# Attention scores in matmuls of 512 and 256 columns instead of 384, and a later ready time for TensorE's operands in the planner

## The chip, the core and the metric

The kernel runs on one core of a Trainium2 chip. The metric is the device time of one execution in microseconds (us). The profile names the engines PE (TensorE matmuls), PEld (TensorE weight loads), DVE (VectorE), ACT (ScalarE), POOL (GpSimd) and SP (SyncE, which issues DMAs). PSUM, where matmuls write, is one array of 8 banks of 512 fp32 columns here, called `banks`.

## What is computed

Attention of 24,576 queries (two batches of 12,288) over 768 keys each, which are 4x4 averages of `kv` times `w_sr`; keys and values are the same. Two feed-forward layers follow, the first with ELU, the second with squared ReLU, both 128 -> 2048 -> 128.

```python
kv_pool = kv.reshape(B, H // r, r, W // r, r, C).mean(axis=(2, 4))
k = v = kv_pool.reshape(B, -1, C) @ w_sr          # 2 x 768 x 128
s = scale * (q @ k.transpose(0, 2, 1))
a = exp(s - s.max(-1)); a /= a.sum(-1) + 1e-09
x = a @ v
h = x @ w_in;  g = where(h > 0, h, exp(min(h, 0)) - 1);  y = g @ w_out
h = maximum(y @ w_in2, 0);  out = h * h @ w_out2
```

## The kernel before

The queries are cut into 48 blocks t of 512 tokens (24 in each batch). To keep fp32 accuracy, each large product is done as three matmuls of a type named fp32r: an operand is split into a high part (…H) and a low part (…L), and `products` (lines 262 to 266) does L*H, H*H and H*L, each with 512 columns, into one PSUM bank. High parts are mostly made by ACT, low parts by DVE as the difference.

For each block the steps are:

- **scores(t, s)**, s = 0 to 3: 128 queries against 768 keys, six matmuls (lines 485 to 492) into banks 0 and 1, 384 columns in each bank. The pair of banks is the only place for scores after the first block. Then `row_max` (DVE, line 495), `exps` (ACT, line 499), `recip` (DVE), `normalise` (ACT for even s, POOL for odd s), `turn` (DVE, line 517). When the four are turned, `move` (16 DMAs on SP's queue, line 558) brings the probabilities into `pL`.
- **values(t, j)**, j = 0 to 2: `p_hi` (ACT, line 568) copies a third of `pL` to `turned` as the high part, `p_lo` (DVE, line 572) leaves the low part in `pL`; then six matmuls of 512 columns each (line 574). Of each three, the first two read `turned`, the third reads `pL`. The result is split into xH and xL.
- **hidden(0, t, i)** and **down(0, t, i)**, i = 0 to 15: the first layer, three matmuls of 512 columns each, 0.68 us. Between them `exp` (ACT, line 620), `less_one` (POOL, line 623), `pick` (DVE, line 627), and for each pair of i a split into gH (ACT, line 631) and gL (DVE, line 634).
- **hidden(1, t, i)** and **down(1, t, i)**: the second layer, with `relu` and `square` on ACT, the high part sH on POOL (line 658), the low part sL on DVE (line 662). It runs about two blocks behind the first layer, so that PE alternates between steps of both layers, of scores and of values. A step is one such group of matmuls.

No loop sets the order. `Program.order` (lines 57 to 132) draws up, before anything is issued, one list of all steps by simulating the five engines with a table of costs; each engine then runs its steps in that list's order. A step is ready when the last of its operands is done plus a latency of the producing engine (`LATENCY`, line 25). Each engine takes, among its 24 most urgent steps, the most urgent one, unless another could start over 10 ns earlier. Buffers, PSUM banks included, are kept apart from that: a place is free when its last reader is done (`free`). Line 127 is where the finish of a step (`done`, the latency included) becomes the ready time of its users. The planner's list also holds filler matmuls (line 733) where PE would idle long; all of them stand in the opening.

The keys of a batch are made by `make_keys`: six matmuls of 128 columns for kH/kL and six for vH/vL, and a split of each in two halves of 384 columns (lines 400 to 416).

Of the kernel before, what the change touches and what calls it, by code (L numbers as in the profile page):

```python
# [11 lines left out]
F32R = mybir.dt.float32r  # L12
# [17 lines left out]
class Program:  # L30
# [26 lines left out]
    def order(self, kinds, fill=None):  # L57
# [30 lines left out]
        while any(queue.values()):  # L88
# [47 lines left out]
def kernel(  # L136
# [26 lines left out]
    NB = 512  # L163
    NS = NB // P
    NKEY = (HH // R) * (WW // R)
    KH = NKEY // 2
    NKC = NKEY // P
    NF = DFF // P
    BPB = N // NB
# [44 lines left out]
    kinds["scores0"] = [(("bank", i), ("bank", i + 1)) for i in range(0, 8, 2)]  # L214
    ring("pooled", 1, [P, NKEY])
    for tag in ("kH", "kL", "vH", "vL"):
        ring(tag, 1, [P, 2, KH], F32R)
    ring("prob", 3, [P, NKEY])
    ring("turned", 1, [P, NKC, NB], F32R)
    ring("pL", 1, [P, NKC, NB], F32R)  # L220
# [167 lines left out]
    def make_keys(b, due):  # L388
        kept = [("keep", b, t) for t in range(NKC)]

        def make(x, due):
            ps, hi, lo = (x + "ps", b), (x + "H", b), (x + "L", b)
            scale = SCALE if x == "k" else 1.0

            def chunk(c):
                dst = v_chunk(buf(*ps), c)
# [6 lines left out]
            def lo_half(h):  # L403
                nc.vector.scalar_tensor_tensor(
                    out=buf(*lo)[:, h, :], in0=buf(*ps)[:, h, :KH], scalar=scale, in1=f32(buf(*hi)[:, h, :]),
                    op0=ALU.mult, op1=ALU.subtract,
                )
# [11 lines left out]
        make("v", due + 1000)  # L419

    def v_chunk(x, c):
        return x[:, c // 3, (c % 3) * C:(c % 3 + 1) * C]

# [8 lines left out]
    def pieces(x, a):  # L432
        return x[32 * a:32 * (a + 1), :].rearrange("p (g i) -> p g i", i=32)

    def by_half(x):
        return x.rearrange("p (h c) n -> p h c n", h=2)

    def of_chunks(x):
        return x[:, :, :KH].rearrange("p h (c n) -> p h c n", n=P)

    def split(tag, t, ps, cost, due, after):

# [8 lines left out]
    def attention(t, base):  # L451
# [30 lines left out]
        def softmax(s, due):  # L482
            k = (t, s)

            def scores():
                x = [a[:, s * P:(s + 1) * P] for a in parts("qT", t)]
                ps, kH, kL = buf("scores", *k), buf("kH", b), buf("kL", b)
                for h in range(2):
                    nc.tensor.matmul(ps[:, h, :KH], x[0], kH[:, h, :], start=True, stop=False)  # L489
                    nc.tensor.matmul(ps[:, h, :KH], x[0], kL[:, h, :], start=False, stop=False)  # L490
                for h in range(2):
                    nc.tensor.matmul(ps[:, h, :KH], x[1], kH[:, h, :], start=False, stop=True)  # L492

            def row_max():
                nc.vector.tensor_reduce(out=buf("max", *k), in_=buf("scores", *k)[:, :, :KH], op=ALU.max, axis=AX.XY,
                                        negate=True)

            def exps():
                nc.scalar.activation(  # L499
                    buf("prob", *k).rearrange("p (h k) -> p h k", h=2), buf("scores", *k)[:, :, :KH], AF.Exp,  # L500
                    bias=buf("max", *k), accum_out=buf("sum", *k),
                )

# [17 lines left out]

            def p_transpose():
                for c in range(NKC):
                    nc.tensor.transpose(v_chunk(buf("pps", *k), c), buf("prob", *k)[:, c * P:(c + 1) * P], ident)

            def p_hi():
                nc.scalar.copy(by_half(buf("pH", t))[:, :, :, s * P:(s + 1) * P], of_chunks(buf("pps", *k)))

            def p_lo():
                nc.vector.tensor_sub(by_half(buf("pL", t))[:, :, :, s * P:(s + 1) * P], of_chunks(buf("pps", *k)),  # L530
                                     by_half(f32(buf("pH", t)))[:, :, :, s * P:(s + 1) * P])

            done = [("qTH", t), ("qTL", t)]
            if t % BPB == BPB - 1:
# [236 lines left out]
```

## Time and profile before

| | |
|---|---|
| median of 3 runs | 2573.49 us (2572.44 to 2574.39) |
| profiled execution, its own time | 2575.82 us |
| span of that execution | 2574.0 us |
| PE busy | 2558.7 us (99%), 11,636 matmul records |
| DVE, ACT, POOL busy | 2280.9 (89%), 2103.8 (82%), 1343.5 (52%) us |

The recorded length of a matmul is longer than its turn: a 512-column matmul is recorded as 0.39 us long while the next one starts 0.23 us after it, so busy time alone doesn't show whether PE loses time. The distance from the start of one matmul to the start of the next does. A fp32 matmul that is not fp32r, such as those of the keys, has two records.

### The profile page before, as it was taken

The numbers are of one execution on the slowest core, as the hardware profiler recorded it, in microseconds if no ns is written. First come the engines' busy times: TensorE is split into PE (matmuls) and PEld (weight loads), VectorE is DVE, ScalarE is ACT, GpSimd is POOL, SyncE is SP. The second block draws the span as 40 slices with busy tenths as digits, with TensorE's granted clock in tenths as the row PEclk, the third lists the DMA queues.
The fourth block names the chain that finished last, engine by engine and source line by source line (L and its number), as shares of the span: only waits on it lengthen the run. The fifth ranks groups of instructions, "written<-read, shape, count | busy, mean of one in ns | idle before, by whom it ended". The sixth has DMA issues, their size and how long they took to land.

```text
span 2574.0 us, 35216 instructions
## 1 busy us (share of the span) xinstructions
PE 2558.7 (99%) x11636; PEld 2136.3 (83%) x11636; DVE 2280.9 (89%) x2700; ACT 2103.8 (82%) x3138; POOL 1343.5 (52%) x1318
## 2 busy tenths in 40 slices
PE   9999999999999999999999999999999999999999
PEld 8888888888888888888888888888888888888887
DVE  4999989999899899998899989999999899988985
ACT  5888878888788888888888878888888888887886
POOL 3655545555566556564455545554455445544543
PEclk9999999999999999999999999999999999999999
DMA  8012211122112212121112211121112111211110
GB/s 246 13 33 48 47 34 38 38 59 56 46 41 50 67 45 46 42 61 42 37 34 47 48 34 37 38 57 34 37 33 58 38 38 33 49 43 29 33 30 13
DMA packets 360374, 119.29 MB, mean 46 GB/s; under 512 B 209024, under 2 KB 353024, under 8 KB 360192
## 3 DMA queue, kind: packets, MB, share of 16 engines
q1 hardware_dynamic: 358992, 116.85, 19.3%
q8 instruction: 92, 1.51, 0.3%
q14 instruction: 90, 0.74, 0.1%
q10 hardware_dynamic: 1200, 0.20, 0.0%
HBM read 33.61 MB, written 12.58 MB: 18 GB/s over the span
## 4 chain that ended last, share of the span: by engine, by line
PE 89%; SPq 3%; DVE 3%; DMA 2%; ACT 2%; issue 1%; POOL 0%; ACTq 0%; POOLq 0%; DVEq 0%
PE banks L266 27%; PE banks L265 27%; PE banks L264 27%; SPq L558 3%; PE banks L489 3%; PE banks L490 3%; PE banks L492 3%; DVE sL L662 1%; DMA pL<-turned 1%; DVE gL L634 1%; DVE pL L572 0%; DVE g L627 0%; DMA g<-in_kv_dram 0%; DMA r<-in_moe_w_in_dram 0%; ACT prob L499 0%
## 5 line engine op out<-in xcount | busy, mean ns | idle before, releaser
L623 POOL TENSOR_SCALAR e<-e 128x512 f32<-128x512 f32 x768 | 680.0, 888 | 860.6 <-ACT e L620 859.9
L662 DVE TENSOR_TENSOR sL<-r,sH 128x1024 fp32r<-128x1024 f32 x380 | 596.2, 1569 | 13.5 <-POOL sH L658 12.2
L620 ACT ACTIVATE e<-banks 128x512 f32<-128x512 f32 x768 | 458.7, 599 | 156.6 <-PE banks L266 140.1
L634 DVE TENSOR_TENSOR gL<-g,gH 128x1024 fp32r<-128x1024 f32 x384 | 529.0, 1378 | 59.1 <-ACT gH L631 54.2
L627 DVE SCALAR_TENSOR_TENSOR g<-e,banks 128x512 f32<-128x512 f32 x768 | 507.1, 674 | 78.1 <-POOL e L623 76.1
L658 POOL TENSOR_SCALAR sH<-r 128x1024 fp32r<-128x1024 f32 x380 | 411.2, 1082 | 261.1 <-PE banks L265 202.0
L652 ACT ACTIVATE r<-banks 128x512 f32<-128x512 f32 x768 | 462.6, 603 | 64.2 <-DVE sL L662 29.6
L631 ACT CAST gH<-g 128x1024 fp32r<-128x1024 f32 x384 | 404.3, 1053 | 78.0 <-PE banks L265 41.6
L655 ACT ACTIVATE r<-r 128x1024 f32<-128x1024 f32 x384 | 409.7, 1067 | 10.7
L264 PE MATMUL banks<-xH,wi0L 128*128 128x512 f32 x768 | 300.9, 392 | 0.0
L264 PE MATMUL banks<-yH,wi1L 128*128 128x512 f32 x768 | 300.8, 392 | 0.0
L266 PE MATMUL banks<-gL,wo0H 128*128 128x512 f32 x768 | 299.9, 391 | 0.8 <-DVE gL L634 0.8
L266 PE MATMUL banks<-xL,wi0H 128*128 128x512 f32 x768 | 300.4, 391 | 0.0
L264 PE MATMUL banks<-gH,wo0L 128*128 128x512 f32 x768 | 299.5, 390 | 0.7 <-DVE g L627 0.7
L265 PE MATMUL banks<-xH,wi0H 128*128 128x512 f32 x768 | 299.9, 391 | 0.0
L265 PE MATMUL banks<-gH,wo0H 128*128 128x512 f32 x768 | 299.6, 390 | 0.0
L266 PE MATMUL banks<-yL,wi1H 128*128 128x512 f32 x768 | 299.4, 390 | 0.0
L265 PE MATMUL banks<-yH,wi1H 128*128 128x512 f32 x768 | 299.4, 390 | 0.0
L266 PE MATMUL banks<-sL,wo1H 128*128 128x512 f32 x760 | 297.1, 391 | 0.0
L265 PE MATMUL banks<-sH,wo1H 128*128 128x512 f32 x760 | 296.6, 390 | 0.0
L264 PE MATMUL banks<-sH,wo1L 128*128 128x512 f32 x760 | 295.6, 389 | 0.0
L512 POOL TENSOR_SCALAR prob<-prob,rcp 128x768 f32<-128x768 f32 x102 | 190.9, 1871 | 60.1 <-DVE rcp L506 54.9
(132 smaller groups left out, 4348.6 us busy)
## 6 DMA issues: line engine op xcount, KB each, us to landing
pL<-turned SPq DMA_DIRECT2D x720, 96.0 KB, 2.2
out_dram<-o SPq DMA_DIRECT2D x190, 64.0 KB, 1.9
q<-in_q_dram SPq DMA_DIRECT2D x180, 64.0 KB, 2.3
ld<-in_kv_dram SPq DMA_DIRECT2D x32, 256.0 KB, 3.6
g<-in_kv_dram SPq DMA_DIRECT2D x8, 256.0 KB, 6.8
gH<-in_kv_dram SPq DMA_DIRECT2D x8, 256.0 KB, 6.9
r<-in_moe_w_in_dram SPq DMA_DIRECT2D x3, 511.8 KB, 7.3
ld<-in_moe_w_in_dram SPq DMA_DIRECT2D x3, 511.8 KB, 4.2
```

Of the source, the lines that this page charges most:

```text
L264: nc.tensor.matmul(dst, lhs[1], rhs[0], start=start, stop=False)
L265: nc.tensor.matmul(dst, lhs[0], rhs[0], start=False, stop=False)
L266: nc.tensor.matmul(dst, lhs[0], rhs[1], start=False, stop=stop)
L620: nc.scalar.activation(buf("e", *k), buf(*h), AF.Exp)
L623: nc.gpsimd.tensor_scalar(out=buf("e", *k), in0=buf("e", *k), scalar1=-1.0, scalar2=1.0, op0=ALU.add, op1=ALU.mult)
L627: nc.vector.scalar_tensor_tensor(out=buf("g", *pair)[:, i % 2, :], in0=buf("e", *k), scalar=0.0, in1=buf(*h), op0=ALU.min, op1=ALU.max)
L631: nc.scalar.copy(buf("aH", 0, *pair), buf("g", *pair))
L634: nc.vector.tensor_sub(buf("aL", 0, *pair), buf("g", *pair), f32(buf("aH", 0, *pair)))
L652: nc.scalar.activation(buf("r", *pair)[:, i % 2, :], buf(*h), AF.Relu)
L655: nc.scalar.activation(buf("r", *pair), buf("r", *pair), AF.Square)
L658: nc.gpsimd.tensor_scalar(out=buf("aH", 1, *pair), in0=buf("r", *pair), scalar1=1.0, scalar2=1.0, op0=ALU.mult, op1=ALU.mult)
L662: nc.vector.tensor_sub(buf("aL", 1, *pair), buf("r", *pair), f32(buf("aH", 1, *pair)))
```

## The change

Three edits. The first: `scores` now covers the 768 keys in columns 0 to 511 (bank 0) and 512 to 767 (bank 1), with three matmuls each. They are still six matmuls, 2304 columns in all and six weight loads; the third of the six is now the first to read the low part of the queries (before it was the fifth). What reads scores (`row_max`, `exps`, and in the first three blocks `p_hi`, `p_lo`) reads 768 columns that follow each other, where it read two runs of 384. The second: kH, kL, vH, vL are flat arrays of 768 columns, and are split in parts of 512 and 256 columns, whose ACT and DVE steps wait for four and for two key chunks instead of three and three. The third: in the planner, for steps that start after 130 us of its own clock, an operand from another engine counts for PE as ready 400 ns later. It is an edit of the list alone; no wait is added to the program. The costs in the table are as they were.

```diff
+BULK, AHEAD = 130000.0, 400.0
@@ order
             for u in users.get(n, ()):
-                ready[u] = max(ready[u], now[e] + SAME[e] if self.ops[u][0] == e else done)
+                early = AHEAD if start > BULK and self.ops[u][0] == "pe" and e != "pe" else 0.0
+                ready[u] = max(ready[u], now[e] + SAME[e] if self.ops[u][0] == e else done + early)
@@ make_keys
             def hi_half(h):
-                nc.scalar.activation(buf(*hi)[:, h, :], buf(*ps)[:, h, :KH], AF.Copy, scale=scale)
+                x = spans[h]
+                nc.scalar.activation(buf(*hi)[:, x], flat(buf(*ps))[:, x], AF.Copy, scale=scale)
...
-                op((x + "_hi", b, h), "act", 370, due, partial(hi_half, h), [(x, b, 3 * h + i) for i in range(3)])
+                op((x + "_hi", b, h), "act", 370, due, partial(hi_half, h), [(x, b, c) for c in range(4 * h, min(4 * h + 4, NKC))])
...
+    spans = (slice(0, NB), slice(NB, NKEY))
@@ scores
-                ps, kH, kL = buf("scores", *k), buf("kH", b), buf("kL", b)
-                for h in range(2):
-                    nc.tensor.matmul(ps[:, h, :KH], x[0], kH[:, h, :], start=True, stop=False)
-                    nc.tensor.matmul(ps[:, h, :KH], x[0], kL[:, h, :], start=False, stop=False)
-                for h in range(2):
-                    nc.tensor.matmul(ps[:, h, :KH], x[1], kH[:, h, :], start=False, stop=True)
+                ps, kH, kL = flat(buf("scores", *k)), buf("kH", b), buf("kL", b)
+                for y in spans:
+                    nc.tensor.matmul(ps[:, y], x[0], kH[:, y], start=True, stop=False)
+                    nc.tensor.matmul(ps[:, y], x[0], kL[:, y], start=False, stop=False)
+                    nc.tensor.matmul(ps[:, y], x[1], kH[:, y], start=False, stop=True)
```

How the list moves is seen at three places. Line numbers of the changed kernel are one higher in `products` (265 to 267) and four or five higher further down (scores 494 to 496, exps 503, gH 635). Numbers behind a name tell buffers of one kernel apart and mean nothing across the two.

PE, block 16, around values(16, 0), whose matmuls read `turned` and `pL`. Before:

```order
L264 MATMUL banks<-sH_8073,wo1L 128x512
L265 MATMUL banks<-sH_8073,wo1H 128x512
L266 MATMUL banks<-sL_8090,wo1H 128x512
L264 MATMUL banks<-turned_8140,vL_314 128x512
L265 MATMUL banks<-turned_8140,vH_313 128x512
L266 MATMUL banks<-pL_8021,vH_313 128x512
L264 MATMUL banks<-turned_8140,vL_314 128x512
L265 MATMUL banks<-turned_8140,vH_313 128x512
L266 MATMUL banks<-pL_8021,vH_313 128x512
L264 MATMUL banks<-xH_7702,wi0L 128x512
L265 MATMUL banks<-xH_7702,wi0H 128x512
L266 MATMUL banks<-xL_7708,wi0H 128x512
```

The same place in the changed kernel:

```order
L265 MATMUL banks<-sH_8073,wo1L 128x512
L266 MATMUL banks<-sH_8073,wo1H 128x512
L267 MATMUL banks<-sL_8090,wo1H 128x512
L265 MATMUL banks<-xH_7706,wi0L 128x512
L266 MATMUL banks<-xH_7706,wi0H 128x512
L267 MATMUL banks<-xL_7712,wi0H 128x512
L265 MATMUL banks<-turned_8140,vL_314 128x512
L266 MATMUL banks<-turned_8140,vH_313 128x512
L267 MATMUL banks<-pL_8021,vH_313 128x512
```

A step of hidden(0, 15, ·) now stands ahead of values(16, 0). The same shift by one step stands in block 3, blocks 11 to 22 and blocks 24 to 47; in blocks 4 to 10 values(t, 0) comes nine places later and in block 23 thirteen, with p_hi and p_lo moved later too. In the other blocks p_hi and p_lo keep their places on ACT and DVE.

PE, block 17, around scores(17, 1), which stands behind a step of down(0, 15, ·). Before:

```order
L264 MATMUL banks<-gH_8169,wo0L 128x512
L265 MATMUL banks<-gH_8169,wo0H 128x512
L266 MATMUL banks<-gL_8191,wo0H 128x512
L489 MATMUL banks<-kH_240,qTH_7918 128x384
L490 MATMUL banks<-kL_241,qTH_7918 128x384
L489 MATMUL banks<-kH_240,qTH_7918 128x384
L490 MATMUL banks<-kL_241,qTH_7918 128x384
L492 MATMUL banks<-kH_240,qTL_7962 128x384 x2
```

The same place in the changed kernel:

```order
L494 MATMUL banks<-kH_240,qTH_7916 128x512
L495 MATMUL banks<-kL_241,qTH_7916 128x512
L496 MATMUL banks<-kH_240,qTL_7962 128x512
L494 MATMUL banks<-kH_240,qTH_7916 128x256
L495 MATMUL banks<-kL_241,qTH_7916 128x256
L496 MATMUL banks<-kH_240,qTL_7962 128x256
L265 MATMUL banks<-gH_8172,wo0L 128x512
L266 MATMUL banks<-gH_8172,wo0H 128x512
L267 MATMUL banks<-gL_8194,wo0H 128x512
```

The scores are in 512 and 256 columns, and stand ahead of the step that they stood behind; scores(t, 0) and scores(t, 1) do so in blocks 4 to 23.

ACT, block 17, around exps(17, 0), which frees the two banks for scores(17, 1). Before:

```order
L620 ACTIVATE e_8228<-banks 128x512
L631 CAST gH_8242<-g_8167 128x1024
L499 ACTIVATE prob_8221,sum_8253<-banks,max_8237 128x768
L620 ACTIVATE e_8264<-banks 128x512
L652 ACTIVATE r_8219<-banks 128x512
```

The same place in the changed kernel:

```order
L624 ACTIVATE e_8233<-banks 128x512
L503 ACTIVATE prob_8216,sum_8241<-banks,max_8228 128x768
L635 CAST gH_8251<-g_8164 128x1024
L514 ACTIVATE prob_8216<-prob_8216,rcp_8256 128x768
L624 ACTIVATE e_8275<-banks 128x512
```

exps(17, 0) now stands ahead of the cast of gH, and normalise(17, 0) right behind that. In all, 412 of 3502 steps on PE stand elsewhere, all but the values by three places or fewer; on DVE 506, on ACT 445, on POOL 32. The last blocks' end and the 37 fillers are in the same places.

## Rows read from the trace of the kernel before

**Rows 1.** The page: busy time of each engine; TensorE's granted clock in 40 slices.

```profile
PE 2558.7 (99%) x11636; PEld 2136.3 (83%) x11636; DVE 2280.9 (89%) x2700; ACT 2103.8 (82%) x3138; POOL 1343.5 (52%) x1318
...
PEclk9999999999999999999999999999999999999999
```

**Rows 2.** Stretch: length, busy PE, PEld, DVE, ACT, POOL, clock, DMA share, GB/s.

```profile
1500.00:2000.00 500.00, 499.83 (x2242) 416.99 (x2241) 453.57 (x538) 415.83 (x615) 254.46 (x251) 1.00 0.19 42
```

**Rows 3.** Timeline, PE, 999 to 1012 us: start, length, instruction; 52 rows between.

```profile
999.82 0.39 PE L265 MATMUL banks<-yH,wi1H 128*128 128x512 f32 x1
...
1011.83 0.39 PE L264 MATMUL banks<-turned,vL 128*128 128x512 f32 x1
```

**Rows 4.** Timeline, PE, one tile of scores and nine matmuls behind it.

```profile
1242.89 0.33 PE L489 MATMUL banks<-kH,qTH 128*128 128x384 f32 x1
...
1243.95 0.39 PE L264 MATMUL banks<-sH,wo1L 128*128 128x512 f32 x1
...
1246.03 0.39 PE L264 MATMUL banks<-gH,wo0L 128*128 128x512 f32 x1
```

**Rows 5.** Timeline, PE, the opening: two tiles of scores (twelve matmuls) back to back.

```profile
33.49 0.34 PE L489 MATMUL banks<-kH,qTH 128*128 128x384 f32 x1
...
35.57 1.28 PE L733 MATMUL banks<-ident 128*128 128x128 f32 x10
```

**Rows 6.** Timeline, PE: runs of 12 records of 128 columns, and what follows.

```profile
29.49 1.50 PE L398 MATMUL banks<-wsr,pooled 128*128 128x128 f32 x12
30.83 0.60 PE L464 MATMUL banks<-ident,q 128*128 128x128 f32 x4
...
1219.86 1.50 PE L398 MATMUL banks<-pooled,wsr 128*128 128x128 f32 x12
...
1221.89 0.39 PE L264 MATMUL banks<-sH,wo1L 128*128 128x512 f32 x1
```

**Rows 7.** Timeline, PEld and PE: scores(11, 3), which waited; a load's recorded length.

```profile
556.25 0.19 PEld L489 LDWEIGHTS banks<-kH,qTH 128*128 128x128 f32 x1 [0.73 <-ACT prob L499]
...
556.36 0.19 PEld L490 LDWEIGHTS banks<-kL,qTH 128*128 128x128 f32 x1
```

**Rows 8.** Who waited for whom: engine, tile, line <- releaser: us, times, longest us.

```profile
PEld banks L266 <- DVE pL L572: 9.5, 16, 1.0
...
PEld banks L489 <- ACT prob L499: 6.3, 9, 1.1
```

**Rows 9.** Timeline, PE, values(44, 0): the last of the sixteen waits for pL.

```profile
2311.54 0.49 PE L264 MATMUL banks<-turned,vL 128*128 128x512 f32 x1
2311.87 0.40 PE L265 MATMUL banks<-turned,vH 128*128 128x512 f32 x1
2312.80 0.50 PE L266 MATMUL banks<-pL,vH 128*128 128x512 f32 x1 [0.53 <-DVE pL L572]
2313.14 0.40 PE L264 MATMUL banks<-turned,vL 128*128 128x512 f32 x1
```

**Rows 10.** Timeline, block 16: ACT's p_hi and DVE's p_lo ahead of values(16, 0).

```profile
846.85 1.05 ACT L568 CAST turned<-pL 128x1024 fp32r<-128x1024 f32 x1 [1.45 <-DMA pL<-turned]
...
847.92 1.23 DVE L572 TENSOR_TENSOR pL<-pL,turned 128x1024 fp32r<-128x1024 f32 x1 [2.09 <-ACT turned L568]
```

**Rows 11.** Timeline, ACT, then PE, block 17: exps(17, 0) and scores(17, 1).

```profile
858.82 1.05 ACT L631 CAST gH<-g 128x1024 fp32r<-128x1024 f32 x1 [0.93 <-PE banks L265]
...
860.56 0.19 ACT L499 ACTIVATION_READ_ACCUMULATOR prob<-banks,max 128x1 f32 x1
...
861.59 0.33 PE L489 MATMUL banks<-kH,qTH 128*128 128x384 f32 x1
```

**Rows 12.** Groups of instructions: count, busy us, mean ns, idle time ahead and its releaser.

```profile
L495 DVE TENSOR_REDUCE max<-banks 128x1 f32<-128x768 f32 x192 | 181.4, 945 | 23.8 <-PE banks L492 22.2
...
L499 ACT ACTIVATE prob<-banks,max 128x768 f32<-128x768 f32 x192 | 173.5, 904 | 39.0 <-DVE max L495 38.9
...
L266 PEld LDWEIGHTS banks<-xL,wi0H 128*128 128x128 f32 x768 | 144.2, 188 | 30.9 <-DVE xL L445 0.7
```

More of the change, by code (lines that the diff above doesn't have):

```diff
@@ L165 @@
     NKEY = (HH // R) * (WW // R)
-    KH = NKEY // 2
     NKC = NKEY // P
@@ L216 @@
     for tag in ("kH", "kL", "vH", "vL"):
-        ring(tag, 1, [P, 2, KH], F32R)
+        ring(tag, 1, [P, NKEY], F32R)
     ring("prob", 3, [P, NKEY])
@@ L395, in chunk @@
             def chunk(c):
-                dst = v_chunk(buf(*ps), c)
+                dst = v_chunk(flat(buf(*ps)), c)
                 keys = buf("pooled", b)[:, c * P:(c + 1) * P]
@@ L400, in hi_half @@
             def hi_half(h):
-                nc.scalar.activation(buf(*hi)[:, h, :], buf(*ps)[:, h, :KH], AF.Copy, scale=scale)
+                x = spans[h]
+                nc.scalar.activation(buf(*hi)[:, x], flat(buf(*ps))[:, x], AF.Copy, scale=scale)
             def lo_half(h):
+                x = spans[h]
                 nc.vector.scalar_tensor_tensor(
-                    out=buf(*lo)[:, h, :], in0=buf(*ps)[:, h, :KH], scalar=scale, in1=f32(buf(*hi)[:, h, :]),
+                    out=buf(*lo)[:, x], in0=flat(buf(*ps))[:, x], scalar=scale, in1=f32(buf(*hi)[:, x]),
                     op0=ALU.mult, op1=ALU.subtract,
@@ L419, in make_keys, with flat @@
         make("v", due + 1000)
+    def flat(x):
+        return x.rearrange("p a n -> p (a n)")
+    spans = (slice(0, NB), slice(NB, NKEY))
     def v_chunk(x, c):
-        return x[:, c // 3, (c % 3) * C:(c % 3 + 1) * C]
+        return x[:, c * C:(c + 1) * C]
     G = P // 32
@@ L433, in pieces @@
         return x[32 * a:32 * (a + 1), :].rearrange("p (g i) -> p g i", i=32)
-    def by_half(x):
-        return x.rearrange("p (h c) n -> p h c n", h=2)
     def of_chunks(x):
-        return x[:, :, :KH].rearrange("p h (c n) -> p h c n", n=P)
+        return flat(x)[:, :NKEY].rearrange("p (c n) -> p c n", n=P)
     def split(tag, t, ps, cost, due, after):
@@ L486, in scores @@
                 x = [a[:, s * P:(s + 1) * P] for a in parts("qT", t)]
-                ps, kH, kL = buf("scores", *k), buf("kH", b), buf("kL", b)
-                for h in range(2):
-                    nc.tensor.matmul(ps[:, h, :KH], x[0], kH[:, h, :], start=True, stop=False)
-                    nc.tensor.matmul(ps[:, h, :KH], x[0], kL[:, h, :], start=False, stop=False)
-                for h in range(2):
-                    nc.tensor.matmul(ps[:, h, :KH], x[1], kH[:, h, :], start=False, stop=True)
+                ps, kH, kL = flat(buf("scores", *k)), buf("kH", b), buf("kL", b)
[3 more added lines that the diff above has]
+                    nc.tensor.matmul(ps[:, y], x[1], kH[:, y], start=False, stop=True)
             def row_max():
-                nc.vector.tensor_reduce(out=buf("max", *k), in_=buf("scores", *k)[:, :, :KH], op=ALU.max, axis=AX.XY,
+                nc.vector.tensor_reduce(out=buf("max", *k), in_=flat(buf("scores", *k))[:, :NKEY], op=ALU.max, axis=AX.X,
                                         negate=True)
@@ L499, in exps @@
                 nc.scalar.activation(
-                    buf("prob", *k).rearrange("p (h k) -> p h k", h=2), buf("scores", *k)[:, :, :KH], AF.Exp,
+                    buf("prob", *k), flat(buf("scores", *k))[:, :NKEY], AF.Exp,
                     bias=buf("max", *k), accum_out=buf("sum", *k),
@@ L523, in p_transpose @@
                 for c in range(NKC):
-                    nc.tensor.transpose(v_chunk(buf("pps", *k), c), buf("prob", *k)[:, c * P:(c + 1) * P], ident)
+                    nc.tensor.transpose(v_chunk(flat(buf("pps", *k)), c), buf("prob", *k)[:, c * P:(c + 1) * P], ident)
             def p_hi():
-                nc.scalar.copy(by_half(buf("pH", t))[:, :, :, s * P:(s + 1) * P], of_chunks(buf("pps", *k)))
+                nc.scalar.copy(buf("pH", t)[:, :, s * P:(s + 1) * P], of_chunks(buf("pps", *k)))
             def p_lo():
-                nc.vector.tensor_sub(by_half(buf("pL", t))[:, :, :, s * P:(s + 1) * P], of_chunks(buf("pps", *k)),
-                                     by_half(f32(buf("pH", t)))[:, :, :, s * P:(s + 1) * P])
+                nc.vector.tensor_sub(buf("pL", t)[:, :, s * P:(s + 1) * P], of_chunks(buf("pps", *k)),
+                                     f32(buf("pH", t))[:, :, s * P:(s + 1) * P])
             done = [("qTH", t), ("qTL", t)]
```

## Prediction

> **What bounds the kernel now.** I read the busy times first: PE is at 99%, its granted clock at the top level in all slices, so 2.4 GHz throughout [rows 1]. The middle of the run says the same: in 500 us PE is busy for 499.83, DVE for 453.57 and ACT for 415.83, so these two have 9% and 17% to spare [rows 2]. Busy time hides small losses, so I went on to starts. In an undisturbed stretch 53 matmuls of 512 columns take 1011.83 - 999.82 = 12.01 us, or 226.6 ns each [rows 3]: that is PE's pace, and time can be won only where starts lie further apart. Two such places repeat. One is each tile of scores. The other is the list of waits, where PE's loader waits 16 times for `pL` and 9 times for `exps` to free the score banks [rows 8].
>
> **Scores: what a tile costs.** Two tiles in a row take 35.57 - 33.49 = 2.08 us for twelve matmuls: 173.3 ns for 384 columns [rows 5]. Between the two paces lie (226.6 - 173.3) / 128 = 0.416 ns a column; carried on, a 256-column matmul takes 173.3 - 53.3 = 120 ns. A tile would be 6 x 173.3 = 1.04 us before and 3 x 226.6 + 3 x 120 = 1.04 us after: the same columns, the same number of matmuls, no gain. But a tile in the stream isn't at that pace. It takes 1243.95 - 1242.89 = 1.06 us, and the nine 512-column matmuls behind it take 1246.03 - 1243.95 = 2.08 us where nine at pace take 2.04 [rows 4]. So a change of length between matmuls costs about 0.02 + 0.04 = 0.06 us a tile, and 192 tiles lose 11.5 us. What the trace doesn't show is this surplus for 256 columns. Its neighbours: a run of twelve 128-column records, at 1.34 / 12 = 112 ns each, with three 512-column matmuls behind it takes 2.03 us, where 1.34 + 3 x 0.227 = 2.02 are due, so about 0.01 [rows 6]; for 384 columns it is 0.06. 256 lies midway, and I take 0.04: the change saves 0.02 x 192 = **3.8 us**. The bounds: the surplus goes (-11.5 us), or it doubles (+11.5 us), since the step from 512 to 256 is twice as large as that to 384.
>
> **Does a load hide behind 256 columns?** Each matmul has its own weight load. Behind a wait, loads start 556.36 - 556.25 = 0.11 us apart [rows 7], and 128-column records with a load each come every 112 ns [rows 6]. So a load needs about 0.11 us, a matmul of 256 columns gives it 0.12, and 0.01 is left. The Trainium skill ("TensorE: Matmul & The Clock Gate", section "LDWEIGHTS (loading the stationary operand)") gives columns over 1.2 as a load's time in ns, 107 for 128 columns, and the trace agrees with its 0.11. By the streaming rate of 2.4 columns per ns alone, 256 columns too take 107 ns as an estimate, which would leave such a load no cover to spare.
>
> **The list: values.** The wait for `pL` is seen best at values(44, 0): the third matmul starts 0.93 us behind the second instead of 0.23, so 0.70 late, and the matmul before and behind it each lose 0.10 or 0.11, since a load is exposed [rows 9]. The chain behind it is the probabilities' DMA, then p_hi for 1.05 us on ACT, then p_lo on DVE [rows 10]; DVE and ACT had waited, so they aren't late by their own queue. The sixteen waits are 9.5 us of the loader's idle time [rows 8]. Normally a load starts one matmul ahead, about 0.23, and leaves 0.04 idle; PE's own loss is 9.5 - 16 x 0.27 + 16 x 0.11 = 6.9 us. In the changed list a step of three matmuls stands ahead, 3 x 0.2266 = 0.68 us, while p_hi and p_lo keep their places. The worst case was late by about 0.70, so hardly more than 0.02 stays at each of the worst three. In blocks 4 to 10 and 23 nine or more steps move ahead, and p_lo moves back by four places on DVE, of 0.7 to 1.6 us each; that also nets a later consumer. I take **6.5 us** of the 6.9. It can't be more than 6.9 plus the first matmul of the worst few, 7.5; it is zero if PE waits for something else instead.
>
> **What else is moved.** The 9 waits for `exps` (0.73 at scores(11, 3)) [rows 7, 8] are waits for banks, which the new term doesn't touch; scores(t, 3) has the same neighbours in blocks 11 to 21. I leave them as they are: zero. Scores(t, 1) of blocks 4 to 23 moves a step ahead. Before, exps(17, 0) ended at 860.75 and scores(17, 1) began at 861.59 [rows 11], a margin of 0.84; 0.68 earlier leaves 0.16, and a load that wants to start 0.23 ahead would miss it by up to 0.1. But scores(t, 0) moves ahead as well, and exps(17, 0) now stands before the cast of gH, which itself waited for 0.93 us [rows 11]. So the margin stays: zero, at worst 20 x 0.1 = 2 us. What is queued behind exps on ACT is that cast, and behind the cast gL and a down step; ACT has the time [rows 2]. Row_max (945 ns) and exps (904 ns) read the same 768 columns [rows 12]: zero either way. In the opening, kH, kL, vH and vL have the same columns in two pieces; scores(0, 0) needs the low part of the queries two matmuls earlier; I put the opening at zero, with 0.5 us to both sides. DMAs keep their number; on SP's queue 16 steps change place by one, at no cost that I can see.
>
> **The sum.** -3.8 - 6.5 = -10.3 us. The profiled execution took 2575.82 us, 1.8 more than its span, so 2565.5 for a like execution. The median of the runs is 2.33 lower than that execution, which gives **2563 us**, 0.4% less.
>
> **The rivals.**
> - **Both terms at their best.** The first three matmuls of a tile now have the stream's own length, so the surplus may go whole: -11.5 - 6.9 gives 2555 us. For it: the 128-column run, hardly disturbed [rows 6]. Against: the exit from 256 to 512 columns is still there.
> - **The list nets nothing.** In blocks 4 to 10, values now end about 2.4 us (two steps and a tile of scores) ahead of hidden(0, t, 0), which needs xH and xL from ACT and DVE; in blocks 11 to 21 of the kernel before the distance was about 2.0, and all waits for xL together were 0.7 us [rows 12], which speaks against. Or DMA's lateness simply shows one step later. Scores alone are left: 2573.5 - 3.8 = 2570 us.
> - **Slower: the short matmul costs more than its columns.** Its load is recorded as 0.19 us long [rows 7], more than 0.12. If the 256-column matmul can't come sooner than midway between 0.12 and the 0.173 of 384 columns, 576 of them cost 0.0265 x 576 = 15.3 us more at an unchanged surplus: 2573.5 - 6.5 + 15.3 = 2582 us. It eats the list's gain from 0.120 + 6.5 / 576 = 0.131 us on, and is slower by over 0.2% from 0.14. Against it: 384 columns at 0.173 are also shorter than the recorded 0.19, and 128-column records come at 0.112.
> - **The waits don't sit in the list.** If the edit to the planner moves steps by less than the chip's scatter, only scores count; the time is that of the second rival, and its chance is in there.
>
> **How the numbers follow.** Forecast 47%, best case 15%, the list nets nothing 26%, slower 12%. About 0.2%, 5 us, can be told from no change. So faster (below 2568) 0.62, same 0.26, slower (above 2579) 0.12. The range: 2554 at the low end holds nearly all of the best case; at the high end 2577 takes in the forecast with the surplus doubled and half the list's gain lost, 2563 + 15 = 2578, nearly. About 2 in 10 are left out.
>
> **What would show it.** Right: scores tiles of about 1.04 us with 256-column starts 0.12 apart, the nine matmuls behind at 2.04 to 2.08; the loader's wait for `pL` under 1 us in sum and not replaced; the 9 waits for `exps` still there; the opening's end within 0.5 us. Wrong: 256-column starts 0.14 apart or more, or a new row of PE waiting for xL, gL or `exps` with as many us as `pL` had.

## The result, and the profile after

The changed kernel takes 2588.12 us (median of 5 runs, 2586.15 to 2590.28) where the kernel before, on the same chip, takes 2574.39: a ratio of 1.0054, with an interval of 1.004 to 1.0068. It is 13.7 us slower. The forecast was 2563 us, and the time lies above the whole range. The profiled execution of the changed kernel took 2590.28 us, its span is 2588.5.

The busy times hardly tell it. This is the page of the changed kernel: busy time and share of each engine, and below it the shares of the chain that ended last.

```profile
PE 2560.9 (99%) x11636; PEld 2104.8 (81%) x11636; DVE 2286.3 (88%) x2700; ACT 2106.9 (81%) x3138; POOL 1323.9 (51%) x1318
...
PE 74%; DVE 9%; SPq 5%; issue 3%; ACT 3%; DMA 2%; POOL 2%; ACTq 0%; POOLq 0%; DVEq 0%
```

No engine does more than 6 us more than in [rows 1], and PE is again at 99%. The chain tells more: PE's own share of it is 74%. In the kernel before it was 89%:

```profile
PE 89%; SPq 3%; DVE 3%; DMA 2%; ACT 2%; issue 1%; POOL 0%; ACTq 0%; POOLq 0%; DVEq 0%
```

Where that share falls, PE is released by others more often.

The middle of the run, 1500 to 2000 us, with the columns of [rows 2]:

```profile
1500.00:2000.00 500.00, 498.98 (x2239) 409.64 (x2238) 452.66 (x542) 413.79 (x615) 253.53 (x250) 1.00 0.18 40
```

The granted clock is at the top level (1.00) as before, so 2.4 GHz. PE is now idle for 1.02 us of these 500, where it was 0.17. That is still little, because a record is longer than its matmul's turn.

The waits of the changed kernel say where PE is held. First the loader's list, then PE's own (engine, tile, line <- releaser: us, times, longest us):

```profile
PEld banks L494 <- ACT prob L503: 15.8, 27, 1.0
PEld banks L265 <- ACT turned L572: 12.4, 11, 1.9
PEld banks L265 <- ACT r L656: 11.9, 25, 1.2
PEld banks L265 <- DVE g L631: 6.7, 24, 0.4
...
PE banks L265 <- DVE g L631: 8.6, 11, 1.5
PE banks L494 <- ACT prob L503: 6.7, 13, 0.7
```

The wait for `pL` (9.5 us, sixteen times [rows 8]) is gone from the list, as the edit wants. In its place stand two new kinds: waits at line 265, the first matmul of a group of three, and three times as many waits for `exps` at line 494.

**The loss in us.** Starts of matmuls measure it better than idle time. For every pair of successive matmuls from hidden(0, 2, 14) on, I took the distance of their starts less the pace of the first (226.67 ns for 512 columns, 173.33 for 384, 120 for 256). A surplus of more than 45 ns is counted as a wait, under the step that came late; what is below that is the column "small". "Opening" is the time until hidden(0, 2, 14) starts. All in us, from the profiled execution of each kernel; in brackets the blocks in which it occurs.

| | opening | values(t, 0) | scores(t, 2), (t, 3) | other waits | small |
|---|---|---|---|---|---|
| before | 163.0 | 7.8 (16) | 3.5 (6) | 3.6 | 12.6 |
| after | 164.2 | 20.4 (44) | 10.5 (12) | 3.1 | 6.7 |
| difference | +1.2 | +12.6 | +7.0 | -0.5 | -5.9 |

The sum is +14.4 us, and the last matmul of PE starts 2583.49 - 2569.04 = 14.45 us later: the table leaves nothing out. The change did two things that were foreseen (the small distances shrank, the waits for `pL` left the loader's list) and two that were not.

### The profile page after: what moved, and what is told of

Same layout as the page of the kernel before. It is cut to its first block, busy times and chain, and to the rows that moved or that the text cites. A ratio compares the mean times of both kernels' runs of the same rounds, so it can differ in the third digit from the quotient of the medians.

```text
span 2588.5 us, 35222 instructions
## 1 busy us (share of the span) xinstructions
PE 2560.9 (99%) x11636; PEld 2104.8 (81%) x11636; DVE 2286.3 (88%) x2700; ACT 2106.9 (81%) x3138; POOL 1323.9 (51%) x1318
## 4 chain that ended last, share of the span: by engine, by line
PE 74%; DVE 9%; SPq 5%; issue 3%; ACT 3%; DMA 2%; POOL 2%; ACTq 0%; POOLq 0%; DVEq 0%
PE banks L265 23%; PE banks L266 23%; PE banks L267 23%; SPq L562 5%; DVE sL L666 3%; PE banks L494 2%; PE banks L496 2%; DVE g L631 2%; PE banks L495 2%; DVE gL L638 2%; DMA pL<-turned 1%; DVE max L499 1%; POOL e L627 1%; ACT e L624 1%; ACT turned L572 1%
## 5 line engine op out<-in xcount | busy, mean ns | idle before, releaser
L666 DVE TENSOR_TENSOR sL<-r,sH 128x1024 fp32r<-128x1024 f32 x380 | 588.9, 1550 | 13.4 <-POOL sH L662 13.4
L638 DVE TENSOR_TENSOR gL<-g,gH 128x1024 fp32r<-128x1024 f32 x384 | 539.7, 1406 | 45.3 <-ACT gH L635 40.8
L659 ACT ACTIVATE r<-r 128x1024 f32<-128x1024 f32 x384 | 409.8, 1067 | 10.7
L503 ACT ACTIVATE prob<-banks,max 128x768 f32<-128x768 f32 x192 | 173.7, 905 | 47.7 <-DVE max L499 47.6
```

Source lines behind the costliest of these rows:

```text
L638: nc.vector.tensor_sub(buf("aL", 0, *pair), buf("g", *pair), f32(buf("aH", 0, *pair)))
L659: nc.scalar.activation(buf("r", *pair), buf("r", *pair), AF.Square)
L666: nc.vector.tensor_sub(buf("aL", 1, *pair), buf("r", *pair), f32(buf("aH", 1, *pair)))
```

## What happens at values(t, 0)

The timeline of the changed kernel in block 16, engine by engine: ACT, DVE, then PE (start, length, instruction, and idle time before it with its releaser; x2 stands for two instructions):

```profile
853.91 1.05 ACT L572 CAST turned<-pL 128x1024 fp32r<-128x1024 f32 x1 [1.23 <-DMA pL<-turned]
...
854.99 1.23 DVE L576 TENSOR_TENSOR pL<-pL,turned 128x1024 fp32r<-128x1024 f32 x1 [1.87 <-ACT turned L572]
856.13 1.28 DVE L631 SCALAR_TENSOR_TENSOR g<-e,banks 128x512 f32<-128x512 f32 x2
...
855.32 0.39 PE L267 MATMUL banks<-xL,wi0H 128*128 128x512 f32 x1
856.96 0.47 PE L265 MATMUL banks<-turned,vL 128*128 128x512 f32 x1 [1.26 <-DVE g L631]
```

The first matmul of values(16, 0) reads `turned`, which p_hi (line 572) has had ready since 854.96. It starts at 856.96, after p_lo (line 576) and, of the two `pick` in the next row (line 631), the first. The kernel before, in the same block, ACT and then PE:

```profile
843.70 0.60 ACT L652 ACTIVATE r<-banks 128x512 f32<-128x512 f32 x1
...
847.95 0.50 PE L264 MATMUL banks<-turned,vL 128*128 128x512 f32 x1 [0.20 <-ACT turned L568]
...
849.21 0.50 PE L266 MATMUL banks<-pL,vH 128*128 128x512 f32 x1 [0.53 <-DVE pL L572]
```

There the first matmul waited for `turned` and started at 847.95, while p_lo was still running (847.92 to 849.15 [rows 10]), and the third waited again, for `pL`. In order of the program, with the semaphores that each instruction waits on, the same matmul reads, before and after:

```
L264 MATMUL banks_83<-turned0_8140,vL0_314 128x512 [waits Activation_49]
L265 MATMUL banks_83<-turned0_8140,vL0_314 128x512 [waits DVE_49,Activation_49]
```

The new DVE wait is for the PSUM bank. The planner gives each step the bank that by its own clock became free first. Before, values(16, 0) got the bank of hidden(1, 14, 1), whose reader `relu` stands two places ahead of p_hi on ACT: it is the first row above, done at 844.30, and p_hi starts at 846.85 [rows 10]. Now a step of hidden(0, 15, ·) stands in front of values(16, 0) and takes that bank. Values(16, 0) gets the next, which hidden(0, 15, 13) used. That bank's last reader is a `pick`, and this `pick` stands right behind p_lo on DVE. DVE runs in its list's order, so the `pick`, whose own input POOL had finished at 852.05, waits with p_lo for the probabilities' DMA and runs from 856.13 to 856.81; and PE waits for the `pick`. In all 44 blocks values(t, 0) starts 0.14 to 0.15 us after that `pick` ends. So a step was put ahead to give p_lo time, and with it the whole group came to depend on what stands *behind* p_lo. Blocks 3 to 22 do this with hidden(0, t-1, 13), blocks 24 to 47 with hidden(0, t-1, 11).

The planner did not see it because the 400 ns count for operands alone: `ready` gets them, `free`, which times the banks, doesn't. A bank is taken as free at the planner's nominal time.

## The experiments

The theory was the one above, and for scores that an exchange on DVE makes exps(t, 1) late. The rivals: the 256-column matmuls cost more than their columns; the list's shift by itself leaves PE waiting for xL behind values; or the probabilities' DMA simply comes later. Times are medians, and ratios are to the kernel before on the same chip.

**The two halves of the change, each alone.** The shapes without the planner's term, and the planner's term with the old shapes:

```diff
-BULK, AHEAD = 130000.0, 400.0
+BULK, AHEAD = 130000.0, 0.0
```

> The 512/256 columns alone: the added term is 0, so PE, POOL and SP run the list of before; only four steps on ACT and two on DVE in the opening differ. Theory A (the list costs, the columns gain): from the third block on, the changed kernel's trace has 5.9 us less of small distances in and behind the tiles of scores than before, so about 2574 - 6 = 2568 us, up to 2570 if the opening is 1.2 us longer as in the changed kernel; the 16 waits for pL are back at about 7.8 us, scores(t, 3) at 3.5. Theory B (the short matmuls, or reading 768 columns that follow each other, cost): about 2588 us or at least above 2574.

```diff
+BULK, AHEAD = 130000.0, 400.0
...
+                early = AHEAD if start > BULK and self.ops[u][0] == "pe" and e != "pe" else 0.0
+                ready[u] = max(ready[u], now[e] + SAME[e] if self.ops[u][0] == e else done + early)
```

> The planner's 400 ns alone, scores in 384 columns as before: the list of the changed kernel but for six steps in the opening. Theory A: the list costs 13.2 + 5.9 = 19 us in the trace of the changed kernel, so about 2593 us; the waits ahead of values(t, 0) sum to about 20 us and those ahead of scores(t, 3) to 9. Theory B (the columns cost): at or below 2574 us.

The shapes alone take 2569.75 us, ratio 0.998 (0.9971 to 0.999), 4.8 us less than the 2574.59 of the kernel before on this chip. The list alone takes 2592.78, ratio 1.007 (1.0055 to 1.0085), 18.2 more. The two add up: -4.8 + 18.2 = +13.4, and both together gave +13.7. In the profiled execution of the shapes alone the waits at values(t, 0) are also 3.6 us less than before and the other waits 2.7 more, with PE's order unchanged, so the 4.8 us aren't the small distances alone. PE's order in the first is that of the kernel before, in the second that of the changed one, step for step, so the halves are clean. In the table's terms the shapes bring the small distances from 12.6 to 6.0 us; the list brings values to 19.6 us in 44 blocks, scores to 9.2. The loader's list of the kernel with the list alone:

```profile
PEld banks L491 <- ACT prob L501: 15.3, 27, 1.1
PEld banks L266 <- ACT r L654: 12.0, 25, 1.4
PEld banks L266 <- ACT turned L570: 11.7, 11, 1.6
```

These are the rows of the changed kernel, with 384 columns. The short matmul is not their cause. That rival falls.

**Only the `pick` moved.** In the finished list of the changed kernel, on DVE, the `pick` right behind p_lo(t, 0) is put ahead of it (45 blocks); PE and ACT keep their order, and every bank stays where it was:

```diff
+PICKS = 1
...
+        names = [n for _, n in result]
+        for t in range(3, 48):
+            low = ("p_lo", t, 0)
+            after = [n for n in names[names.index(low):] if self.ops[n][0] == "dve"][1:3]
+            for n in after[:PICKS]:
+                if n[0] != "pick" or not self.shift(names, where, n, low):
+                    break
...
```

`shift` (added, not shown) puts a step ahead of another in the list, and leaves the list as it is where an operand or a buffer doesn't allow it.

> The changed kernel, with one swap on DVE in each of 45 blocks: the pick behind p_lo(t, 0) is put ahead of it. Theory A1 (values(t, 0) now takes the bank of a hidden(0, t-1, .) step whose last reader is that pick, and the pick stands behind p_lo(t, 0), which waits for the probabilities' DMA): the bank is free early, values(t, 0) waits for p_lo alone with a step more of time; its 20.4 us of waits fall to 1 to 4 us, so about 2588 - 17 = 2571 us. Theory A2 (the DMA is later in the changed list, whatever the bank): the waits stay near 20 us, 2588 us, or worse by the 0.65 us that p_lo gives up in 45 blocks.

2569.16 us, ratio 0.998 (0.9971 to 0.999): 19.0 less than the changed kernel. Values(t, 0) falls from 20.4 us to 0.1. PE in block 16 of this kernel, with its p_lo:

```profile
846.96 1.23 DVE L597 TENSOR_TENSOR pL<-pL,turned 128x1024 fp32r<-128x1024 f32 x1 [1.00 <-ACT turned L593]
...
847.56 0.39 PE L288 MATMUL banks<-xL,wi0H 128*128 128x512 f32 x1
847.79 0.39 PE L286 MATMUL banks<-turned,vL 128*128 128x512 f32 x1
848.02 0.39 PE L287 MATMUL banks<-turned,vH 128*128 128x512 f32 x1
848.24 0.49 PE L288 MATMUL banks<-pL,vH 128*128 128x512 f32 x1
```

The first matmul follows at 0.23 us while p_lo is still running, and the third, which needs p_lo, starts at 848.24 without loss. This is the gain that the step ahead was to bring. PE's order is that of the changed kernel and the 20 us are gone, so a later DMA was not their cause. The loader's list:

```profile
PEld banks L515 <- ACT prob L524: 15.7, 27, 1.0
PEld banks L286 <- DVE g L652: 8.2, 28, 0.5
PEld banks L288 <- DVE gL L659: 1.6, 3, 1.2
```

The 24 us that stood under `turned` (ACT) and `r` (ACT) are gone, though neither of those was touched. Both names were wrong: the wait was for several semaphores, and the list puts it under one.

**Values put back in place.** In the same blocks values(t, 0) is exchanged with the step ahead of it on PE, and the two exchange their banks:

```diff
...
+            h = pe[pe.index(v) - 1]
+            x, y = ("xps", t), ("h", *h[1:])
...
+            where[x], where[y] = where[y], where[x]
+            if not self.shift(names, where, v, h):
...
```

> The changed kernel, with values(t, 0) put back ahead of the hidden step before it on PE in 44 blocks, and the two steps' banks exchanged, so that values(t, 0) takes the bank freed by a relu as in the kernel before. Theory A1: the waits ahead of values(t, 0) fall from 20.4 to about the 7.8 us of before, so about 2588 - 12.6 = 2575.5 us; those ahead of scores(t, 2) and (t, 3), 10.5 us, stay. Theory A2 (the DMA is later): they stay at 20 us or more, since values now has a step less of time, 2588 us or more.

2581.32 us, ratio 1.0025 (1.0014 to 1.0035), 6 us above the first expectation. Values(t, 0) costs 6.3 us in 13 blocks, near the 7.8 in 16 of the kernel before. But hidden(0, t, ·) now costs 10.1 us, of which 7.5 are 24 waits of 0.31 at hidden(0, t-1, 15), each in its own block, and the loader's list has a row that no other kernel has, xL as the releaser of a first matmul:

```profile
PEld banks L518 <- ACT prob L527: 15.7, 27, 1.0
PEld banks L289 <- DVE xL L474: 11.2, 24, 0.5
PEld banks L291 <- DVE pL L600: 8.4, 14, 0.9
```

The bank that this step takes was last read by the split into xL on DVE. So undoing the shift gives back 6.8 of the 13.7 us, and what it costs elsewhere shows the same thing at another place: every exchange of two steps also exchanges whose reader frees the bank.

**Scores.** In the changed list exps(t, 0) and normalise(t, 0) come earlier on ACT, so turn(t, 0) comes earlier on DVE. In blocks 3 to 23 it now stands ahead of row_max(t, 1), in 13 of them (3 and 11 to 22) directly ahead; the 12 blocks that wait are 11 to 22. The timeline of the changed kernel, block 17, from there to scores(17, 3):

```profile
871.94 0.97 DVE L521 STREAM_TRANSPOSE turned<-prob 128x768 f32<-128x768 f32 x1
872.84 0.91 DVE L499 TENSOR_REDUCE max<-banks 128x1 f32<-128x768 f32 x1
...
873.78 0.90 ACT L503 ACTIVATE prob<-banks,max 128x768 f32<-128x768 f32 x1 [0.86 <-DVE max L499]
...
875.75 1.57 DVE L638 TENSOR_TENSOR gL<-g,gH 128x1024 fp32r<-128x1024 f32 x1
877.24 1.62 DVE L666 TENSOR_TENSOR sL<-r,sH 128x1024 fp32r<-128x1024 f32 x1
878.79 0.94 DVE L499 TENSOR_REDUCE max<-banks 128x1 f32<-128x768 f32 x1
...
879.77 0.90 ACT L503 ACTIVATE prob<-banks,max 128x768 f32<-128x768 f32 x1 [0.86 <-DVE max L499]
...
880.81 0.50 PE L494 MATMUL banks<-kH,qTH 128*128 128x512 f32 x1 [0.56 <-ACT prob L503]
881.15 0.39 PE L495 MATMUL banks<-kL,qTH 128*128 128x512 f32 x1
```

Turn takes 0.97 us, row_max starts behind it, exps(17, 1) waits for row_max, then the cast of gH, gL, sL and the next row_max follow on two queues, each behind the other, and exps(17, 2) is late for scores(17, 3). Before, this gL started 0.36 us after the start of scores(17, 2), now 0.91. The same is tried alone: row_max put back ahead of turn, in 13 blocks, and then together with the `pick`:

```diff
...
+            high = ("row_max", t, 1)
+            last = [n for n in names[:names.index(high)] if self.ops[n][0] == "dve"][-1]
+            if last == ("turn", t, 0):
+                self.shift(names, where, high, last)
...
```

> The changed kernel, with one swap on DVE in 13 blocks: row_max(t, 1) is put ahead of turn(t, 0), as in the kernel before. Theory C1 (turn ahead of row_max makes exps(t, 1) about 0.9 us later; exps stands ahead of gH on ACT, so gL, sL and row_max(t, 2) on DVE and exps(t, 2) come later by half a microsecond, and scores(t, 3) waits for its banks): the waits ahead of scores(t, 2) and (t, 3) fall from 10.5 to about 3.5 us as before, so 2588 - 7 = 2581 us; the values' 20 us stay. Theory C2 (scores(t, 3) waits because its own step or PE's neighbours moved): they stay, 2588 us.

> Both swaps on DVE together, pick ahead of p_lo(t, 0) in 45 blocks and row_max(t, 1) ahead of turn(t, 0) in 13. If the two causes are apart from each other: 2569.2 - 7 = 2562 us, the waits of values near zero and those of scores near 3.5 us; that is faster than the kernel before by 0.5% and about the time that the prediction named. If the waits of scores take the place of those of values, it stays at 2569.

Row_max alone gives 2583.70 us, ratio 1.0037 (1.0023 to 1.005), 4.4 less than the changed kernel. Together with the `pick` it gives 2564.58, ratio 0.9966 (0.9954 to 0.9979): 4.6 less than the `pick` alone (3.6 by the ratios; the two ran on different chips). The waits of scores fall from 10.5 us to 5.7 and 5.8, not to the 3.5 of the kernel before. So the exchange is the cause of about 4.7 of the added 7.0 us. What is left ahead of scores(t, 3) is 0.38 to 0.40 us in the odd blocks, where the kernel before has 0.58 to 0.60, and 0.53 to 0.63 in the even ones, where it has none. Two things still differ from the kernel before. The low part gL starts 0.69 us after scores(t, 2) instead of 0.38. And from there to row_max(t, 2), with gL and sL between on DVE, it takes 3.0 us in the even blocks instead of 2.4 (in the odd ones 2.7 instead of 3.25). Why these times differ stays open.

**The length of matmuls.** The shapes alone again, with the six matmuls in the order 512, 512, 256, 256, 512, 256 columns, so four changes of length a tile where there were two; the columns and the list are the same. The order of the banks changes with it: 0, 0, 1, 1, 0, 1 as in the kernel before, where the shapes alone have 0, 0, 0, 1, 1, 1:

```diff
                 for y in spans:
                     nc.tensor.matmul(ps[:, y], x[0], kH[:, y], start=True, stop=False)
                     nc.tensor.matmul(ps[:, y], x[0], kL[:, y], start=False, stop=False)
+                for y in spans:
                     nc.tensor.matmul(ps[:, y], x[1], kH[:, y], start=False, stop=True)
```

> The columns alone, as in e1, but the six matmuls in the order of before: high parts on 512, 512, 256, 256 columns, then the low part on 512 and 256. The same columns and loads, with two more changes of length in a tile. Theory D1 (a change of length between matmuls costs, in the tile and behind it): the tile and the matmuls behind it take 0.02 to 0.06 us more than in e1, 192 tiles, so 2569.8 + 4 to 2569.8 + 11.5, 2574 to 2581 us. Theory D2 (a change of length costs nothing of its own; before, 384 columns were the cost): the same as e1, 2569.8 us.

2572.64 us, ratio 0.9993 (0.9984 to 1.0003), where the shapes alone had 0.998: about 0.0013 x 2574 = 3.3 us are lost again, though the two intervals overlap. It is less than theory D1 wanted (2574 to 2581) and more than D2 (2569.8). In the trace the small distances go from 6.0 us back to 11.4, and the other waits from 6.3 to 3.7. One tile of this kernel and what follows it:

```profile
859.71 0.39 PE L494 MATMUL banks<-kH,qTH 128*128 128x512 f32 x1
...
860.75 0.40 PE L265 MATMUL banks<-sH,wo1L 128*128 128x512 f32 x1
...
862.85 0.39 PE L265 MATMUL banks<-gH,wo0L 128*128 128x512 f32 x1
```

The tile itself takes 1.04 us. The nine matmuls behind it take 2.10 where nine at pace take 2.04. So the cost appears behind the tile, in the stream. That it is the cost of a change of length isn't shown: D1 and D2 leave out the order of the banks and of the operands, and this run changes that too. Its small distances are close to those of the kernel before (11.4 and 12.6), which has the same order and two changes of length instead of four. For length speaks that in the opening two tiles of 384 columns, in that same order, run at pace [rows 5].

**Banks counted late as well.** If the planner's blindness to banks is the cause, the mending belongs in the planner. The changed kernel with one more term, in which a bank that another engine frees counts 400 ns later too:

```diff
-                through[key] = max(through.get(key, 0.0), done)
+                late = AHEAD if start > BULK and e != "pe" and where[key][0][0] == "bank" else 0.0
+                through[key] = max(through.get(key, 0.0), done + late)
```

> The changed kernel, with the planner's 400 ns also on PSUM banks: a bank freed by ACT or DVE counts as free 400 ns later too. Values(t, 0) then stands a further step of 0.68 us behind the pick that frees its bank. Theory A1: of its 20.4 us of waits only what is above 0.68 us in a block stays, 4 to 5 us; scores(t, 3) stands about a step further behind exps(t, 2), so its 9.3 us fall to under 2; together 2588 - 15 - 8 = 2565 us, if no other wait comes. Theory A2 (later in the list means later on the chip): no change or slower, 2588 us or more.

2568.35 us, ratio 0.9979 (0.9969 to 0.9988): 19.8 less than the changed kernel. Values fall from 20.4 us to 6.4 in 15 blocks, scores stand at 6.4, the small distances at 4.3. The planner, told of the banks, finds by itself as much as the moved `pick` gave.

**One more step ahead of scores(t, 3).** The kernel with both exchanges, and in blocks 11 to 22 the PE step behind scores(t, 3) put ahead of it, to give the last late exps 0.68 us:

```diff
+        for t in range(11, 23):
+            tile = ("scores", t, 3)
+            pe = [n for n in names if self.ops[n][0] == "pe"]
+            self.shift(names, where, pe[pe.index(tile) + 1], tile)
...
```

> e6 with one more swap on PE, in blocks 11 to 22: the hidden step behind scores(t, 3) is put ahead of it, so that exps(t, 2) has 0.68 us more to free the banks. The waits ahead of scores(t, 3) in e6 are 0.28 to 0.46 us each with 0.1 of an exposed load, 5.8 us in 12 blocks. If a step of 0.68 us is all that is missing, they vanish: 2564.6 - 5.5 = 2559 us. If something else comes late behind it (exps(t, 3), then turn and the probabilities' DMA, since scores(t, 3) comes later), it stays at 2564.

2567.43 us, ratio 0.9977 (0.9968 to 0.9987): a miss, 2.9 us slower than without it. The waits of scores did go, from 5.8 us to nothing. But hidden(0, t, ·) went from 2.6 to 8.9 us, six of the waits being of 0.91 to 1.00, at hidden(0, t-1, 5) in even blocks t. PE ahead of scores(20, 3), whose step is hidden(0, 19, 5):

```profile
1027.43 0.39 PE L296 MATMUL banks<-sL,wo1H 128*128 128x512 f32 x1
1028.65 0.50 PE L294 MATMUL banks<-xH,wi0L 128*128 128x512 f32 x1 [0.83 <-ACT r L685]
```

The step that was put ahead waits for its own bank, which relu (line 685, ACT) frees. It is the mistake of the original edit once more, made by hand.

**All together.** Banks counted late, and both exchanges on DVE (41 `pick`, 13 row_max):

> e8, whose planner counts banks late too, with both swaps on DVE: pick ahead of p_lo(t, 0) in 41 blocks, row_max(t, 1) ahead of turn(t, 0) in 13. In e8's trace values(t, 0) still waits 6.4 us in 15 blocks and scores(t, 2) and (t, 3) 6.4 us in 12. If the pick behind p_lo is still what holds the bank, and turn ahead of row_max what makes exps late, about 10 us go: 2568.4 - 10 = 2558 us. If what is left there is the DMA's own lateness, only the 3 to 5 us of scores go: 2564 us.

2557.94 us, ratio 0.994 (0.9925 to 0.9956): 15.2 us less than the kernel before and 30 less than the changed one. Its page, with the shares of its chain, and rows of the loader's list:

```profile
PE 2544.2 (100%) x11636; PEld 2112.4 (83%) x11636; DVE 2286.3 (89%) x2700; ACT 2102.8 (82%) x3138; POOL 1307.7 (51%) x1318
...
PE 95%; DVE 1%; ACT 1%; DMA 1%; SPq 1%; issue 0%; POOL 0%; ACTq 0%; POOLq 0%
```

```profile
PEld banks L520 <- ACT prob L529: 5.7, 8, 0.9
PEld banks L293 <- DVE pL L602: 2.2, 6, 0.6
...
PEld banks L291 <- DVE g L657: 1.5, 5, 0.4
```

PE's share of the chain is 95%, against 74% in the changed kernel. By starts, values(t, 0) cost 0.4 us, scores 3.4, other waits 2.3, the small distances 3.3. By this measure what is left to win behind the opening is under 10 us.

The table of starts for all kernels (us, columns as above; e-numbers in the order in which they stand here):

| | median | values(t, 0) | scores(t, 2), (t, 3) | other waits | small |
|---|---|---|---|---|---|
| e1, shapes alone | 2569.75 | 4.2 | 3.7 | 6.3 | 6.0 |
| e2, list alone | 2592.78 | 19.6 | 9.2 | 1.8 | 13.0 |
| e3, `pick` first | 2569.16 | 0.1 | 10.4 | 4.2 | 4.5 |
| e4, values back | 2581.32 | 6.3 | 10.4 | 10.7 | 5.9 |
| e5, row_max first | 2583.70 | 16.5 | 5.7 | 3.2 | 5.5 |
| e6, both | 2564.58 | 0.1 | 5.8 | 4.4 | 5.0 |
| e7, mixed lengths | 2572.64 | 4.5 | 3.6 | 3.7 | 11.4 |
| e8, banks late | 2568.35 | 6.4 | 6.4 | 2.5 | 4.3 |
| e9, scores later | 2567.43 | 1.9 | 0.0 | 11.7 | 4.9 |
| e10, banks late and both | 2557.94 | 0.4 | 3.4 | 2.3 | 3.3 |

The profiled execution of e5 is 3.4 us below its median, so its row is on the low side. The opening lies between 162.6 and 164.4 us in all of them, with no order by shape: the 1.2 us that it takes longer in the changed kernel can't be put down to the change.

## Why the prediction was wrong

**What bounds the kernel: right.** PE sets the end before and after, and only starts show its losses. But the list of waits [rows 8] was read as if it named all that a step waits for. It names what came last in the kernel before. Who reads the bank last, and behind what, is in no row of waits, only in the order.

**Scores: right in sign, mis-sized.** The surplus of a tile was put at 0.06 us going to 0.04, 3.8 us in all. The shapes alone measured 4.8, and the small distances fell by 6.6 in the trace. The tile in the changed kernel:

```profile
868.34 0.39 PE L494 MATMUL banks<-kH,qTH 128*128 128x512 f32 x1
...
869.02 0.28 PE L494 MATMUL banks<-kH,qTH 128*128 128x256 f32 x1
869.14 0.28 PE L495 MATMUL banks<-kL,qTH 128*128 128x256 f32 x1
869.26 0.28 PE L496 MATMUL banks<-kH,qTL 128*128 128x256 f32 x1
869.38 0.40 PE L265 MATMUL banks<-gH,wo0L 128*128 128x512 f32 x1
...
871.44 0.39 PE L265 MATMUL banks<-yH,wi1L 128*128 128x512 f32 x1
```

It takes 1.04 us against 1.06 in [rows 4], and the nine matmuls behind it 2.06 against 2.08: 0.04 less each tile, not 0.02. The small distances, 5.9 us less, say 0.03 a tile, so the surplus fell by half to two thirds. That a change of length is the cause of the surplus, as the working says, isn't shown (e7).

**The load behind 256 columns: right.** Their starts are 0.12 us apart, as foreseen, and the load stays hidden; the rival by which it wouldn't, with its 2582 us, has the right sign of the result and the wrong cause. The list with the old shapes is slower still, 2592.78 us.

**The list, values: the step that failed.** The working said that a step of 0.68 us ahead of values leaves p_lo time, with p_hi and p_lo in their places, and took 6.5 of 6.9 us as won. The waits for `pL` did go. But the sum knew only the operands of values(t, 0). Values(t, 0) also writes a PSUM bank, and the step in front took the bank that had been its own. The term is +12.6 us, not -6.5. With the `pick` ahead of p_lo the very same list loses 0.1 us there, so the step's premise, that 0.68 us are enough for p_lo, was sound. "The list nets nothing" named xL and the DMA as what could come next. The `pick` was in neither.

**What else is moved: failed as well.** "The 9 waits for `exps` [...] I leave them as they are: zero" became +7.0 us. The text followed ACT, where exps(17, 0) moves ahead of the cast of gH, and found that the margin at scores(t, 1) stays; it does, no wait stands there. It did not follow normalise, which moves with it, to turn on DVE, and turn past row_max(t, 1). Of DVE it knew the 9% to spare [rows 2], and an average says nothing of the order within a queue. The banks were right to be named, and wrong to be left out: "waits for banks, which the new term doesn't touch" is true of the term's text and false of its effect, since the term moves the steps that take and free them.

**The opening, and the sum.** Zero with 0.5 to both sides for the opening is neither borne out nor refuted: it scatters by 1.8 us. The terms come to -3.8 - 6.5 in the prediction and to -5.9 + 12.6 + 7.0 - 0.5 + 1.2 in the trace. With the two exchanges on DVE the changed list measures 2564.58 us, close to the 2563 forecast: it was a forecast for a kernel with the order mended. The closeness is partly luck: against the kernel before, the small distances fell by 7.6 us, not 3.8, and the waits of scores rose by 2.3. At the upper end of the range the sum is wrong too: a doubled surplus alone is 15.3 us above the forecast, and with half the list's gain lost it is 18.6, so 2582 and not 2578; the measured time lies above that as well.

**The signs named in advance** served. "A new row of PE waiting [...] with as many us as `pL` had" is what the loader's list shows at a glance: `exps`, one of the three listed, rose from 6.3 us [rows 8] to 15.8, and `turned` and `r`, which weren't listed, stand at 12.4 and 11.9.

The Trainium skill ("Trainium Kernel Development and Optimization", section "Best Practices") says that bubbles which come back regularly can be a sign that SBUF or PSUM has run out. The trace agrees in part: 44 blocks wait at the same step, 20.4 us in all, for one of the eight banks. But with the `pick` moved the same banks sufficed, at 0.1 us; what was late was the bank's reader.

## What to carry to other kernels

When a list or a scheduler moves a step, write down for each moved step not only who makes its operands but who last reads the buffer it writes, and what that reader stands behind on its own queue. A lateness that a planner counts for operands it must count for buffers too: here the change with operands alone was 13.7 us slower, with both 5.6 us faster, and with two exchanges on DVE besides 15.2. A row of waits names one releaser of several; moving that one alone and seeing whether the row goes is the proof.

## What the runs showed of the hardware

The order of a tile's six matmuls costs time in the stream behind it, though columns and loads are the same. The small distances, over the 176 tiles from block 4 on, count everything small and so are an upper bound: 6.0 / 176 = 34 ns a tile for 512, 512, 512, 256, 256, 256 columns (e1), 11.4 / 176 = 65 ns for 512, 512, 256, 256, 512, 256 (e7). The kernel before, with 384 columns in e7's order of banks, has 12.6 / 176 = 72 ns. The runs don't tell whether the changes of length cost it (two, four and two of them) or the order of banks and operands that e7 shares with the kernel before. I had expected the larger step in length to cost more, or in between; with the new order it costs half. Why is open.

A 256-column matmul hides its weight load in the stream, with starts of 0.113 to 0.120 us, while behind a wait a load is exposed: the second start comes 0.34 us after the first, which has 512 columns (880.81 and 881.15 in the changed kernel), 0.11 more than the pace.
